# The last inverse stage on tiles of 64 rows and 32 columns, in half units

## The chip, the cores and the metric

The kernel runs on one core of a Trainium2 chip. The metric is the device time of one execution in microseconds (us). A core has a TensorE (PE, matrix products, with its weight loads shown apart as PEld), a VectorE (DVE), a ScalarE (ACT), a GpSimd (POOL) and a SyncE (SP), which here does nothing but issue DMAs. All run their own instructions in order and wait for each other by semaphores.

## The reference

One layer on 2048 tokens (L) of 640 channels (D). First a long convolution whose kernel comes from a diagonal state-space model (N = 128 states for each channel), then a gated feed-forward network (F = 1728), each behind a layer norm with a scale and a shift from a condition vector and each added through a gate:

```python
def A(u):                                   # [1, L, D]
    dt = exp(log_dt); A = -exp(log_A_real) + 1j * A_imag; C = (C_real + 1j * C_imag) * dt[:, None]
    K = 2 * einsum("dn,dnl->dl", C, exp((A * dt[:, None])[:, :, None] * pos)).real
    y = irfft(rfft(u.T, 2L) * rfft(K, 2L), 2L)[:, :, :L].T
    return y + u * D_skip
def B(x):
    return (silu(x @ w1) * (x @ w3)) @ w2
sa, ca, ga, sb, cb, gb = split(silu(c) @ w_mod)
x = x + ga * A(layernorm(x) * (1 + ca) + sa)
x = x + gb * B(layernorm(x) * (1 + cb) + sb)
```

Everything is in fp32.

## The kernel before, in words

**First phase (0 to about 395 us).** The convolution is a transform of 4096 points in stages, forward for the tokens and for the generated kernel K, a product, and an inverse transform. Each stage is a set of matmuls with a constant table (`wk`, `wb`, `wz`, `wd`). The channels run in five pieces of 128. The work is cut in tasks, and a list of task numbers, `ORDER`, written out in the file, says in which order they are issued; the costs and due times that stand at the tasks are not read by `run`. The last product of the inverse's first stage, `fz`, is copied by ACT to `zt` and stored by SP to a buffer `zd` in HBM; the last stage reads it back with the other axes in front.

**The last inverse stage.** A token's place is 32 values long in one axis; the 64 positions of the other axis are grouped as `j`, 0 to 15, in four quarters `q`. `inverse_load` fetches `z` for `nj` values of `j` (I call each a token row below): for each of two pairs `pr` a tile whose upper 64 rows are quarter 2·pr and whose lower 64 rows are quarter 2·pr + 1, four DMAs in all. `inverse` then makes, for each token row and each cut of up to 512 columns, one PSUM tile `iy` of 128 rows with two matmuls, one for each pair, on tiles of 128 rows and 64 columns of the array. The table `wd` holds a block diagonal for them: a quarter's 64 rows have values in its own 32 columns and zeros in the 32 of the other quarter. DVE then adds `iy` into `x2`, which holds the layer's input x and, after this, the input of the second half.

All this stands in one SBUF tile `low`: the table, `x2[0]`, and two buffers of `z`, taken in turn by units of two token rows. Units 0 and 1 (token rows 0 to 3) are done in the plan for the first 512 channels, as tasks `iz0`, `iz1` (the loads) and `ir0`, `ir1` (the matmuls, additions and layer norm statistics). Their last 128 channels, four token rows in one load on SP and ACT, follow behind the plan, with `awake` matmuls as a filler for PE around them.

**The feed-forward network.** Blocks 0 and 1 of 512 tokens run in `ffn`, blocks 2 and 3 together in `pair_up` and `pair_down`. A block goes through 14 slices m of F in the order 0, 13, 1, 2, ... 12. For each slice `up` makes two PSUM tiles `gu` (15 matmuls each; the half slice 13 has one tile); `gate` evaluates them on ACT and DVE into `ah`, `al`; `down` adds 15 matmuls into five accumulators `acc`. Each fp32 operand is split in a high and a low part (`wh`, `wl`, `xh`, `xl`, `w2h`, `w2l`), so there are three products where one stood. The weights come by SP as `wr` and `w2r` and are split by ACT and DVE. The tag `gu` has three PSUM banks, shared by `gu` and `iy`.

A function `between(b, m)` is called in each slice and puts other work in among these. For block 0 and m from 2 to 7 it calls `inverse_unit(m)`: the four loads of the unit (token rows 2m and 2m + 1, all 640 channels) and its four `iy` tiles, two cuts of 320 channels for each token row. The framework's scheduler makes PE's order from this program: it may put the accumulations of an earlier slice before, between or behind the `iy` matmuls.

SP issues DMAs in program order; a DMA that must wait for a buffer holds those behind it.

Of the kernel before, what the change touches and what calls it, by code (L numbers as in the profile page):

```python
# [10 lines left out]
F32 = mybir.dt.float32  # L11
# [7 lines left out]
P = 128  # L19
L = 2048  # L20
D = 640
# [76 lines left out]
def shape_tables():  # L98

    slot_t0 = np.array([32 + s if s < 32 else 63 - s for s in range(64)])  # L100
    t1, t0, f0, f1 = np.arange(32), np.arange(64), np.arange(32) + 0.5, np.arange(64)
    w = 2 * np.pi / 4096


    a = w * 64 * t1[:, None] * f0
    wk = np.zeros((4, 32, 2, 4, 32))
    for g in range(4):
        wk[g, :, :, g] = np.stack([np.cos(a), -np.sin(a)], 1)


    def second(a):
        c, s = np.cos(a), np.sin(a)
        return np.concatenate([np.concatenate([c, -s], -1), np.concatenate([s, c], -1)], 0)

    wb = np.stack([second(w * slot_t0[:, None] * (f + 64 * f1)) for f in f0], 1)

    a = w * 64 * f1[:, None] * t0
    c, s = np.cos(a), np.sin(a)
    wz = np.tile(np.stack([np.block([c, s]), np.block([-s, c])], 1), (2, 1, 1))

    wd = np.zeros((2, 32, 2, NJ, 2, 2, 32))
    a = w * (64 * t1[:, None] + t0) * f0[:, None, None]
    st = np.stack([np.cos(a), -np.sin(a)], 1) * 2 / 4096
    for q in range(4):
        wd[q % 2, :, :, :, q // 2, q % 2] = st[..., 16 * q:16 * q + 16].transpose(0, 1, 3, 2)
    return {k: np.ascontiguousarray(v.astype(np.float32)) for k, v in
            (("t_wk", wk.reshape(P, 2, P)), ("t_wb", wb), ("t_wz", wz), ("t_wd", wd.reshape(P, NJ, 2, 64)))}

# [32 lines left out]
class Plan:  # L161
# [4 lines left out]
    def add(self, name, eng, took, f, after=(), rank=0.0, port=False, take=(), give=(), table=None, dma=None):  # L166
        assert name not in self.tasks, name
        if not isinstance(eng, tuple):
            eng, f = (eng,), f and (lambda e, f=f: f())
        self.tasks[name] = (eng, f, tuple(after))  # L170
# [14 lines left out]
class K:  # L185
# [351 lines left out]
    def inverse_load(self, at, j0, nj, d0, d1, other=None):  # L537

        zv = self.zd.rearrange("f r t d -> (f r) t d")
        n = nj * (d1 - d0)  # L540
        z = [self.low[:, o:o + n].rearrange("p (j d) -> p j d", j=nj) for o in (at, at + (1280 if nj == 2 else 512))]
        for pr in range(2):
            for g in range(2):
                t0 = 16 * (2 * pr + g) + j0
                self.held_back((other if g and other else self.nc.sync).dma_start(z[pr][g * 64:(g + 1) * 64], zv[:, t0:t0 + nj, d0:d1]))
        return z

    def inverse(self, j0, nj, z, ps, tag, bufs, d0, d1):
        nc = self.nc
        w = d1 - d0  # L550
        for j in range(nj):
            for o, n in ((0, w),) if w <= 512 else ((0, 320), (320, 320)):
                py = ps.tile([P, 512], F32, name=f"iy{j0 + j}_{d0 + o}", tag=tag, bufs=bufs)
                for pr in range(2):
                    mm = nc.tensor.matmul(py[pr * 64:(pr + 1) * 64, :n], self.wd[:, j0 + j, pr, :], z[pr][:, j, o:o + n],  # L555
                                     start=True, stop=True, tile_position=(0, pr * 64))
                x2 = self.x2[(j0 + j) // 4][:, (j0 + j) % 4, d0 + o:d0 + o + n]
                nc.vector.tensor_add(x2, py[:, :n], x2)
        return mm

    hold = None

    def inverse_unit(self, u, ps, tag, bufs):
        z = self.inverse_load(4608 + u % 2 * 2560, 2 * u, 2, 0, D)
        self.inverse(2 * u, 2, z, ps, tag, bufs, 0, D)


    def split(self, H, Lo, v, eng):
# [483 lines left out]
    def run(self):  # L1052
        real = self.nc
        self.setup()
        c = self.const
# [4 lines left out]
        def open_(name, side=None, bufs=1, space=None):  # L1060
            scopes[name] = ExitStack()
            return self.pool(name, bufs=bufs, space=space, ctx=scopes[name], side=side)

        def close(*names):
            for n in names:
                scopes.pop(n).close()
# [15 lines left out]
        nc = self.nc = Engines(self, real)  # L1082
# [16 lines left out]
        b = NB - 1  # L1099
# [13 lines left out]
        add = plan.add  # L1113
# [5 lines left out]
        z = {}  # L1119
        W = self.W["tail"]  # L1120
# [11 lines left out]
        def load_z(u):  # L1132
            z[u] = self.inverse_load(4608 + u % 2 * 2560, 2 * u, 2, 0, cut)

        def first_rows(u):
            self.inverse(2 * u, 2, z[u], psg, "f", 3, 0, cut)
            for j in (2 * u, 2 * u + 1):
                self.ln_part(self.stats[0], self.x2[0], j, 0, KT - 1)
        for u in range(2):
            add(f"iz{u}", "SP", 0, lambda u=u: load_z(u), ["change", "fx"] + [f"z{b - 1}.{j}.o{f}" for j in range(4) for f in range(2)], W, dma=[262144] * 4)  # L1140
            add(f"ir{u}", "PE", 2.4, lambda u=u: first_rows(u), [f"iz{u}"] + [f"{x}{b}.{i}.e" for x in ("hh", "k") for i in range(8)], W + 25)
        plan.run()
        self.nc = real
# [8 lines left out]
        ps = open_("ps", space=PSUM)  # L1152
        x2 = [keep.tile([P, 4, D], F32, name=f"x2{b}") for b in (2, 3)]
# [3 lines left out]
        z = self.inverse_load(9728, 0, 4, cut, D, real.scalar)  # L1157
# [7 lines left out]
        def between(b, m):  # L1165
            if b == 0 and m in (2, 4):
                self.load_x2(m // 2 + 1)
            if b == 0 and 2 <= m < 8:
                self.inverse_unit(m, ps, "gu", 3)
            if b == 0 and m == 9:  # L1170
                self.gb_row(ps)
            if (b, m) == (1, 0):
                close("lp")
                xc = open_("xc")
                self.px = [xc.tile([P, 2, 2 if i < 5 else 1, 512], F32R, name=f"x3_{i}") for i in range(6)]
            if (b, m) in ((0, 8), (1, 4)):
                nxt[b + 1] = self.ln2(b + 1, pool, ps)
            if (b, m) == (1, 6):
                nxt[3] = self.ln_pair(*nxt[2], pool, ps)
            if b == 1 and 6 <= m < 12:  # L1180
                next(nxt[3])

        pend = self.ffn(nxt, wp, pool, ps, po, between)
        close("conv")
        pool = open_("pair", "right")
# [228 lines left out]
    def spectra_tasks(self, b):  # L1414
# [59 lines left out]
        for i in range(8):  # L1474
            t = W["w"](b, i)
            n = f"w{b}.{i}."
            j = 4 * b + i // 2 - FP
            first = [f"hh{b}.{x}.e" for x in range(8)] + ([f"w{b - 1}.{i}.x1"] if b else ["wb", "cols", "inv"])
            firstk = [f"k{b}.{x}.e" for x in range(8)]
            room = [f"z{j // 4}.{j % 4}.z"] if j >= 0 else []  # L1480
            add(n + "f", "PE", 1.0, lambda i=i: of(0, i), first, t, take=[("bank", 1)])
            add(n + "h", "ACT", .48, lambda i=i: hold(i), [n + "f"], t - q, give=[("bank", n + "f")])
            add(n + "k", "PE", 1.0, lambda i=i: of(1, i), firstk + room, t + .1, take=[("bank", 1)])
            add(n + "x0", "DVE", .61, lambda i=i: product(i, 0), [n + "k", n + "h"] + ([f"w{b}.{i - 1}.x0"] if i % 2 else []), t - q, take=[] if i % 2 else [("fp", 1)])
            add(n + "x1", "DVE", .61, lambda i=i: product(i, 1), [n + "x0"], t - q)
            add(n + "c", "DVE", .67, lambda i=i: both(i), [n + "x1"], t - q, give=[("bank", n + "k")])
            if i % 2 == 0:
                continue
            j = i // 2
            n = f"z{b}.{j}."  # L1490
            add(n + "z", "PE", 1.95, lambda j=j: inverse(j), [f"w{b}.{i - 1}.c", f"w{b}.{i}.c"], t + W["late"], take=[("bank", 1), ("bank", 1, "'")],
                give=[("fp", f"w{b}.{i - 1}.x0")])
            for f in range(2):
                kept = "hz" if (b, j, f) == (NB - 1, 3, 1) else "zt"
                add(n + f"v{f}", ("ACT", "DVE"), (.48, .61), lambda e, j=j, f=f: out(j, f, e), [n + "z"], t - q,
                    take=[(kept, 1)], give=[("bank", n + "z" + "'" * f)])
                add(n + f"o{f}", "SP", 0, lambda j=j, f=f: store(j, f), [n + f"v{f}"], t, dma=[262144], give=[(kept, n + f"v{f}")])
# [272 lines left out]
```

## Time and profile before

| | |
|---|---|
| median of 3 runs | 971.52 us (971.05 to 973.86) |
| the profiled execution, its own time | 970.77 us |
| its span, first to last instruction | 968.8 us |
| its mean granted TensorE clock | 0.966 |
| instructions | 20106 |
| iy matmuls of line 555 (units 2 to 7 and the last 128 columns) on the chain that ended last | 2% of the span |
| DMA, mean over the span | 117 GB/s |

Line 146 is a helper that records every operation of the plan, so groups of the first phase are told apart by their tiles. In timelines and chains each row has its start and its length in us; behind an instruction stand its output and inputs by the program's names, the tile of the array, and the shape; in brackets the idle time of the engine ahead of it and what ended that. An fp32 matmul is two instructions in the profile.

### The profile page before, as it was taken

What the parts mean: (1) busy time and instruction counts of PE and PEld (TensorE: products, weight loads), DVE (VectorE), ACT (ScalarE), POOL (GpSimd) and SP (SyncE); (2) the same over time, 40 slices, a digit from 0 to 9 for tenths busy, and PEclk for the clock granted to TensorE, in tenths of its full rate; (3) what the DMA queues carried; (4) which work ended last, traced back from release to release, by engine and by line L of the source; (5) the groups of instructions that cost most, each with busy time, mean ns of one, the idle gap of its engine ahead of it and who ended that gap; (6) DMA issues with size and microseconds to landing.
All of it is one profiled execution on the core that took longest, in us unless ns stands there. A gap on an engine that the chain in (4) does not pass through costs nothing.

```text
span 968.8 us, 20106 instructions
## 1 busy us (share of the span) xinstructions
PE 860.8 (89%) x8017; PEld 685.6 (71%) x8017; DVE 712.9 (74%) x1292; ACT 517.0 (53%) x874; POOL 336.1 (35%) x345
## 2 busy tenths in 40 slices
PE   2165767899999997899999999999999999999997
PEld 1033655787878773667778888888888888888875
DVE  7888999999999973657684365566467777765763
ACT  5878879979888830523143243345234444445331
POOL 2789998599999530100000000000213223300000
PEclk9585989999999998999999999999999999999999
DMA  9956526624140296987523353223131122122242
GB/s 241 236 175 213 119 59 169 161 68 111 37 99 25 72 276 184 233 203 189 136 82 91 100 148 111 82 82 109 28 82 55 55 54 55 42 82 90 85 152 82
DMA packets 122821, 113.18 MB, mean 117 GB/s; under 512 B 11752, under 2 KB 106472, under 8 KB 121320
## 3 DMA queue, kind: packets, MB, share of 16 engines
q1 hardware_dynamic: 121992, 110.99, 42.6%
q8 instruction: 63, 1.03, 0.5%
q10 hardware_dynamic: 736, 0.92, 0.3%
q14 instruction: 30, 0.25, 0.1%
HBM read 90.91 MB, written 20.97 MB: 115 GB/s over the span
## 4 chain that ended last, share of the span: by engine, by line
PE 66%; DVE 13%; DMA 7%; ACT 6%; issue 3%; POOL 3%; SPq 1%; DVEq 0%; ACTq 0%; POOLq 0%
PE acc L1024 17%; PE p L777 16%; PE gu L987 6%; PE gu L989 6%; PE gu L988 6%; DVE yy L146 3%; DMA xs<-in_x 3%; PE ps L146 2%; PE kps L146 2%; DVE fp L146 2%; ACT tr L146 2%; PE fz L146 2%; DVE xx L146 2%; PE iy L555 2%; DMA sp<-in_w_mod 1%
## 5 line engine op out<-in xcount | busy, mean ns | idle before, releaser
L987 PE MATMUL gu<-xh,wh 128*128 128x512 f32 x270 | 105.0, 394 | 0.9 <-ACT xh L569 0.7
L989 PE MATMUL gu<-xh,wl 128*128 128x512 f32 x270 | 105.4, 390 | 0.0
L988 PE MATMUL gu<-xl,wh 128*128 128x512 f32 x270 | 105.3, 390 | 0.0
L777 PE MATMUL p<-x,wch 128*128 128x512 f32 x312 | 92.7, 390 | 0.0
L796 POOL TENSOR_TENSOR ws<-wp 128x256 f32<-128x256 f32 x13 | 9.6, 739 | 229.8 <-DVE wcl L570 114.9
L146 POOL TENSOR_TENSOR yy<-e,e 128x512 f32<-128x512 f32 x80 | 87.1, 1103 | 3.0 <-PE kps L146 2.3
L146 POOL TENSOR_TENSOR ph<-p,p 128x1024 int32<-128x1024 int32 x40 | 78.5, 1964 | 16.1 <-ACT tr L146 15.7
L146 DVE TENSOR_TENSOR yy<-yy,tr 128x512 f32<-128x512 f32 (+1 forms) x80 | 75.1, 944 | 5.0 <-POOL yy L146 4.6
L681 ACT ACTIVATE wh<-wr 128x640 fp32r<-128x640 f32 x51 | 34.9, 731 | 63.3 <-PE gu L988 54.1
L146 PE MATMUL kps<-yy,xx 128*32 128x64 f32 x2560 | 49.7, 231 | 20.9 <-DVE xx L146 11.5
L777 PEld LDWEIGHTS p<-x,wch 128*128 128x128 f32 x312 | 58.3, 188 | 12.6 <-ACT s L812 0.4
L146 PEld LDWEIGHTS kps<-yy,xx 128*32 128x32 f32 x2560 | 43.4, 115 | 32.8 <-issue 17.0
L987 PEld LDWEIGHTS gu<-xh,wh 128*128 128x128 f32 x270 | 50.6, 188 | 11.7 <-ACT xh L569 1.0
L989 PEld LDWEIGHTS gu<-xh,wl 128*128 128x128 f32 x270 | 50.7, 188 | 11.1 <-DVE wl L690 0.4
L988 PEld LDWEIGHTS gu<-xl,wh 128*128 128x128 f32 x270 | 50.8, 188 | 10.4 <-DVE xl L570 0.2
L693 POOL MEMSET w2l<- 64x640 f32 x1 | 0.6, 633 | 163.7 <-PE acc L1024 163.7
L777 PE MATMUL p<-x,wcl 128*128 128x512 f32 x156 | 57.0, 390 | 0.0
L146 ACT ACTIVATE tr<-ph,hpi 128x512 f32<-128x512 f32 x80 | 54.6, 689 | 3.2 <-DVE yy L146 2.3
L146 DVE TENSOR_TENSOR xx<-tr,xx 128x512 f32<-128x512 f32 x80 | 54.3, 680 | 2.1 <-ACT tr L146 1.9
L814 DVE TENSOR_TENSOR s<-p,s 128x512 f32<-128x512 f32 x52 | 34.7, 682 | 26.9 <-ACT s L812 22.9
L146 PE MATMUL ps<-wk,ks 128*64 128x128 f32 x640 | 42.0, 285 | 13.7 <-DVE ks L146 9.6
L1000 ACT ACTIVATE th<-gu 128x512 f32<-128x512 f32 x26 | 15.5, 598 | 69.9 <-PE gu L989 69.8
(368 smaller groups left out, 2315.9 us busy)
## 6 DMA issues: line engine op xcount, KB each, us to landing
wr<-in_w SPq DMA_DIRECT2D x52, 320.0 KB, 3.8
zd<-zt SPq DMA_DIRECT2D x39, 256.0 KB, 2.7
w2r<-in_w SPq DMA_DIRECT2D x26, 320.0 KB, 3.2
wp<-in_w SPq DMA_DIRECT2D x26, 320.0 KB, 3.5
wq<-in_w SPq DMA_DIRECT2D x26, 320.0 KB, 3.2
low<-zd SPq DMA_DIRECT2D x24, 320.0 KB, 5.9
xs<-in_x SPq DMA_DIRECT2D x16, 320.0 KB, 10.0
hs<-hb SPq DMA_DIRECT2D x20, 256.0 KB, 2.9
```

What stands on the lines that cost most here:

```text
L146: self.prev = self.k.order(f(*a, **kw), self.prev)
L555: mm = nc.tensor.matmul(py[pr * 64:(pr + 1) * 64, :n], self.wd[:, j0 + j, pr, :], z[pr][:, j, o:o + n], start=True, stop=True, tile_positi ...
L681: self.nc.scalar.activation(wh[:, i], raw[:, i], AF.Copy)
L693: self.nc.gpsimd.memset(w2l[64:].bitcast(F32), 0.0)
L777: nc.tensor.matmul(to, t[:, o], y[:, k], start=start and k == i == 0, stop=stop and (k, i) == (n - 1, 2), skip_group_check=True)
L796: G.tensor_tensor(s[0], a21, a22, op=ALU.add)
L814: add = lambda o, bk, s: V.tensor_tensor(o, bk, s, op=ALU.add)
L987: nc.tensor.matmul(pg, wh[:, k, :], xh[:, k, :], start=(k == 0), stop=False)
L988: nc.tensor.matmul(pg, wh[:, k, :], xl[:, k, :], start=False, stop=False)
L989: nc.tensor.matmul(pg, wl[:, k, :], xh[:, k, :], start=False, stop=(k == KT - 1))
L1000: nc.scalar.activation(th, gu[0], AF.Tanh, scale=0.5)
L1024: nc.tensor.matmul(acc[k], *two(a, w), start=(m == 0 and i == 0), stop=(m == 12 and i == 2))
```

## The change

The table `wd` has the same shape, but for odd token rows p its two row halves are exchanged. `inverse_load` fetches even and odd token rows of a quarter apart: the even ones into the row half of before, the odd ones into the other, so eight DMAs of half the size where four stood. `inverse` takes two token rows at a time with a PSUM tile for each, and four matmuls for each tile, one for each quarter, on tiles of 64 rows and 32 columns; the zeros of the table are no longer read. Between them the two token rows use all eight such tiles of the array. The number of additions on DVE is the same.

In `ffn` a unit is done in two halves, one for each cut of 320 channels: half i = m − 2 for m from 2 to 7, i = m − 3 for m from 9 to 13, and the last, i = 11, at m = 0 of block 1. Unit 2 + i // 2 is loaded with its first half. The costs noted at the task of the loads (not read, as said) now name eight DMAs. The lines of the kernel move by 12 or so.

```diff
@@ -122,7 +122,8 @@
     a = w * (64 * t1[:, None] + t0) * f0[:, None, None]
     st = np.stack([np.cos(a), -np.sin(a)], 1) * 2 / 4096
     for q in range(4):
-        wd[q % 2, :, :, :, q // 2, q % 2] = st[..., 16 * q:16 * q + 16].transpose(0, 1, 3, 2)
+        for p in range(2):
+            wd[(q + p) % 2, :, :, p::2, q // 2, q % 2] = st[..., 16 * q + p:16 * q + 16:2].transpose(0, 1, 3, 2)
     return {k: np.ascontiguousarray(v.astype(np.float32)) for k, v in
             (("t_wk", wk.reshape(P, 2, P)), ("t_wb", wb), ("t_wz", wz), ("t_wd", wd.reshape(P, NJ, 2, 64)))}
 
@@ -541,28 +542,39 @@
         z = [self.low[:, o:o + n].rearrange("p (j d) -> p j d", j=nj) for o in (at, at + (1280 if nj == 2 else 512))]
         for pr in range(2):
             for g in range(2):
-                t0 = 16 * (2 * pr + g) + j0
-                self.held_back((other if g and other else self.nc.sync).dma_start(z[pr][g * 64:(g + 1) * 64], zv[:, t0:t0 + nj, d0:d1]))
+                for p in range(2):
+                    t0 = 16 * (2 * pr + g) + j0
+                    to = z[pr][(g ^ p) * 64:(g ^ p) * 64 + 64, p::2]
+                    self.held_back((other if g and other else self.nc.sync).dma_start(to, zv[:, t0 + p:t0 + nj:2, d0:d1]))
         return z
 
-    def inverse(self, j0, nj, z, ps, tag, bufs, d0, d1):
+    def inverse(self, j0, nj, z, ps, tag, bufs, d0, d1, part=None):
+
         nc = self.nc
         w = d1 - d0
-        for j in range(nj):
-            for o, n in ((0, w),) if w <= 512 else ((0, 320), (320, 320)):
-                py = ps.tile([P, 512], F32, name=f"iy{j0 + j}_{d0 + o}", tag=tag, bufs=bufs)
-                for pr in range(2):
-                    mm = nc.tensor.matmul(py[pr * 64:(pr + 1) * 64, :n], self.wd[:, j0 + j, pr, :], z[pr][:, j, o:o + n],
-                                     start=True, stop=True, tile_position=(0, pr * 64))
-                x2 = self.x2[(j0 + j) // 4][:, (j0 + j) % 4, d0 + o:d0 + o + n]
-                nc.vector.tensor_add(x2, py[:, :n], x2)
+        cuts = ((0, w),) if w <= 512 else ((0, 320), (320, 320))
+        for o, n in cuts if part is None else cuts[part:part + 1]:
+            for j in range(0, nj, 2):
+                py = [ps.tile([P, 512], F32, name=f"iy{j0 + j + p}_{d0 + o}", tag=tag, bufs=bufs) for p in range(2)]
+                for p in range(2):
+                    for q in range(4):
+                        r, c = 64 * ((q + p) % 2), 32 * q
+                        mm = nc.tensor.matmul(py[p][c:c + 32, :n], self.wd[r:r + 64, j0 + j + p, q // 2, c % 64:c % 64 + 32],
+                                              z[q // 2][r:r + 64, j + p, o:o + n], start=True, stop=True, tile_position=(r, c))
+                for p in range(2):
+                    i = j0 + j + p
+                    x2 = self.x2[i // 4][:, i % 4, d0 + o:d0 + o + n]
+                    nc.vector.tensor_add(x2, py[p][:, :n], x2)
         return mm
 
     hold = None
 
-    def inverse_unit(self, u, ps, tag, bufs):
-        z = self.inverse_load(4608 + u % 2 * 2560, 2 * u, 2, 0, D)
-        self.inverse(2 * u, 2, z, ps, tag, bufs, 0, D)
+    def inverse_half(self, i, ps, tag, bufs):
+
+        u, h = 2 + i // 2, i % 2
+        if h == 0:
+            self.zu = self.inverse_load(4608 + u % 2 * 2560, 2 * u, 2, 0, D)
+        self.inverse(2 * u, 2, self.zu, ps, tag, bufs, 0, D, h)
 
 
     def split(self, H, Lo, v, eng):
@@ -1137,7 +1149,7 @@
             for j in (2 * u, 2 * u + 1):
                 self.ln_part(self.stats[0], self.x2[0], j, 0, KT - 1)
         for u in range(2):
-            add(f"iz{u}", "SP", 0, lambda u=u: load_z(u), ["change", "fx"] + [f"z{b - 1}.{j}.o{f}" for j in range(4) for f in range(2)], W, dma=[262144] * 4)
+            add(f"iz{u}", "SP", 0, lambda u=u: load_z(u), ["change", "fx"] + [f"z{b - 1}.{j}.o{f}" for j in range(4) for f in range(2)], W, dma=[131072] * 8)
             add(f"ir{u}", "PE", 2.4, lambda u=u: first_rows(u), [f"iz{u}"] + [f"{x}{b}.{i}.e" for x in ("hh", "k") for i in range(8)], W + 25)
         plan.run()
         self.nc = real
@@ -1165,8 +1177,9 @@
         def between(b, m):
             if b == 0 and m in (2, 4):
                 self.load_x2(m // 2 + 1)
-            if b == 0 and 2 <= m < 8:
-                self.inverse_unit(m, ps, "gu", 3)
+            i = m - 2 if m < 8 else m - 3
+            if b == 0 and m >= 2 and m != 8 or (b, m) == (1, 0):
+                self.inverse_half(i if b == 0 else 11, ps, "gu", 3)
             if b == 0 and m == 9:
                 self.gb_row(ps)
             if (b, m) == (1, 0):
```

What the order makes of it is shown at three places. The first is on PE, around 420 us, where the accumulations of slice 13 (`acc` from `ah_13`) end. Before:

```order
L1024 MATMUL acc_5352<-w2h_13_5059,ah_13_5380 128x512
L1024 MATMUL acc_5352<-w2l_13_5077,ah_13_5380 128x512
L555 MATMUL iy_0_5471<-low 64x320 x2
L1024 MATMUL acc_5353<-ah_1_5448,w2h_1_5395 128x512
L1024 MATMUL acc_5349<-w2h_1_5395,ah_1_5448 128x512
L1024 MATMUL acc_5350<-w2h_1_5395,ah_1_5448 128x512
L1024 MATMUL acc_5351<-w2h_1_5395,ah_1_5448 128x512
L1024 MATMUL acc_5352<-w2h_1_5395,ah_1_5448 128x512
L555 MATMUL iy_320_5475<-low 64x320 x2
```

The same place after:

```order
L1036 MATMUL acc_5380<-w2h_13_5067,ah_13_5408 128x512
L1036 MATMUL acc_5380<-w2l_13_5085,ah_13_5408 128x512
L562 MATMUL iy_0_5496<-low 32x320 x3
L999 MATMUL gu_20_5522<-xh_5278,wh_2_5512 128x512
L1000 MATMUL gu_20_5522<-xl_5279,wh_2_5512 128x512
L1001 MATMUL gu_20_5522<-xh_5278,wl_2_5517 128x512
```

Behind the iy matmuls there stood the accumulations of slice 1; now the 30 gu matmuls of slice 2 stand there, and the accumulations of slice 1 come behind them. Of the half unit's eight matmuls the other five stand among those of slice 13.

The second place is on PE too, further on in block 0: where the gu matmuls of slice 3 end, before, and where the accumulations of slice 2 end, after. Before:

```order
L988 MATMUL gu_31_5586<-xl_5251,wh_3_5575 128x512
L989 MATMUL gu_31_5586<-xh_5250,wl_3_5580 128x512
L555 MATMUL iy_0_5649<-low 64x320 x2
L555 MATMUL iy_320_5653<-low 64x320 x2
L555 MATMUL iy_0_5657<-low 64x320 x2
L555 MATMUL iy_320_5661<-low 64x320 x2
L1024 MATMUL acc_5353<-ah_3_5634,w2h_3_5576 128x512
L1024 MATMUL acc_5353<-ah_3_5634,w2l_3_5581 128x512
```

After:

```order
L1036 MATMUL acc_5380<-w2l_2_5518,ah_2_5571 128x512
L1036 MATMUL acc_5380<-w2h_2_5513,al_2_5572 128x512
L562 MATMUL iy_0_5673<-low 32x320 x4
L562 MATMUL iy_0_5674<-low 32x320 x4
L999 MATMUL gu_40_5700<-xh_5278,wh_4_5690 128x512
L1000 MATMUL gu_40_5700<-xl_5279,wh_4_5690 128x512
```

A whole unit of four PSUM tiles stood there in one piece; now a half stands there, with two tiles of four matmuls each, between acc of slice 2 and gu of slice 4.

The third place is SP's queue in the last part of the first phase. `zd<-zt` are the stores, `low<-zd` the loads of units 0 and 1, `wr` and `w2r` the weights of slices 13, 1 and 2. Before:

```order
L146 DMA w2r_13_4930<-in_w 64x640 x2
L146 DMA low<-zd 64x2x512 x4
L665 DMA wr_1_5389<-in_w 128x5x128 x2
L146 DMA zd<-zt_5016 128x4x128
L670 DMA w2r_1_5392<-in_w 128x640
L146 DMA zd<-zt_5027 128x4x128
L146 DMA low<-zd 64x2x512 x4
L665 DMA wr_2_5479<-in_w 128x5x128 x2
L670 DMA w2r_2_5482<-in_w 128x640
L146 DMA zd<-zt_5074 128x4x128
L146 DMA zd<-zt_5114 128x4x128
```

After:

```order
L147 DMA w2r_13_4930<-in_w 64x640 x2
L147 DMA low<-zd 64x512 x8
L677 DMA wr_1_5417<-in_w 128x5x128 x2
L147 DMA zd<-zt_5016 128x4x128
L682 DMA w2r_1_5420<-in_w 128x640
L147 DMA zd<-zt_5031 128x4x128
L147 DMA low<-zd 64x512 x8
L147 DMA zd<-zt_5082 128x4x128
L147 DMA zd<-zt_5126 128x4x128
L677 DMA wr_2_5507<-in_w 128x5x128 x2
L682 DMA w2r_2_5510<-in_w 128x640
```

Each unit's four loads have become eight in the same place, and the weights of slice 2 have moved behind two stores.

## The prediction

> **What bounds the kernel now.** I read the page's first part, then the windows from 416 us on, then the chain of waits there, then single rows of the timeline.
>
> ```profile
> PE 860.8 (89%) x8017; PEld 685.6 (71%) x8017; DVE 712.9 (74%) x1292; ACT 517.0 (53%) x874; POOL 336.1 (35%) x345
> ...
> 416.00:424.00 8.00, 7.04 (x35) 3.66 (x33) 4.09 (x8) 3.25 (x5) 0.00 (x0) 1.00 0.78 199
> 424.00:440.00 16.00, 16.00 (x76) 11.58 (x75) 12.03 (x36) 3.33 (x6) 0.00 (x0) 1.00 0.80 214
> ...
> 460.00:480.00 20.00, 20.00 (x97) 14.28 (x94) 15.90 (x54) 3.70 (x6) 0.00 (x0) 1.00 0.63 165
> ```
>
> The columns of a window are its us, the busy time of PE, PEld, DVE, ACT and POOL with instructions, the granted clock, the DMA share and GB/s. In block 0 (from 424 us) PE is busy for every microsecond, at the full clock; DVE has 4.1 of 20 us to spare where it is fullest. So there a microsecond of PE work taken out moves the end by a microsecond. Just before, from 416 to 424, PE lacks 0.96 us: that is one wait, treated below. The inverse stage stands in this stretch as ten groups of iy matmuls: nine are on the chain of waits, the tenth (four instructions at 420.18) is just ahead of the wait.
>
> ```profile
> 416.49 1.23 PE iy L555 x8
> ...
> 423.33 0.69 PE iy L555 x4
> ...
> 433.35 1.77 PE iy L555 x12
> ...
> 437.63 0.69 PE iy L555 x4
> ...
> 446.52 2.30 PE iy L555 x16
> ...
> 459.24 1.76 PE iy L555 x12
> ...
> 463.52 0.69 PE iy L555 x4
> ...
> 472.41 2.30 PE iy L555 x16
> ...
> 485.14 2.45 PE iy L555 x16
> ```
>
> With those four they are 96 instructions: six units of 16, two instructions for each fp32 matmul.
>
> **Block 0, the PE work.** What a group costs is read from the start of the instruction before it to the start of one behind it, less what those instructions take alone (0.23 us each in the chain, 0.227 from 444.77 to 446.13 over six).
>
> ```profile
> 444.77 0.39 PE L989 MATMUL gu<-xh,wl 128*128 128x512 f32 x1
> ...
> 446.13 0.39 PE L989 MATMUL gu<-xh,wl 128*128 128x512 f32 x1
> 446.45 2.38 PE L555 MATMUL iy<-low 128*64 128x320 f32 x16
> 448.75 0.50 PE L1024 MATMUL acc<-ah,w2h 128*128 128x512 f32 x1
> 449.09 0.40 PE L1024 MATMUL acc<-ah,w2l 128*128 128x512 f32 x1
> ...
> 463.12 0.40 PE L1024 MATMUL acc<-w2l,ah 128*128 128x512 f32 x1
> 463.45 0.76 PE L555 MATMUL iy<-low 128*64 128x320 f32 x4
> 464.14 0.50 PE L1024 MATMUL acc<-al,w2h 128*128 128x512 f32 x1
> 464.48 1.11 PE L1024 MATMUL acc<-w2h,al 128*128 128x512 f32 x4
> ```
>
> A group of 16 costs 449.09 − 446.13 − 2 × 0.227 = 2.51 us, one of 4 costs 464.48 − 463.12 − 0.454 = 0.91. The 128x64 tiles run in pairs, so these are 8 rounds and 2 rounds: a round is (2.51 − 0.91)/6 = 0.267 us, and going into a group and out of it 0.91 − 0.534 = 0.38. Before: 48 rounds and 10 groups, 12.8 + 3.8 = **16.6 us**.
>
> After, a half unit has 8 matmuls on 8 different tiles, again 16 instructions of 320 columns. If all eight run together, that is 2 rounds. The order of after has 13 groups (12 halves, of which unit 2's first is cut in 5 and 3 matmuls), so 26 rounds. Whether eight run together no row shows; the nearest are these:
>
> ```profile
> 269.35 1.17 PE L146 MATMUL kps<-yy,xx 128*32 128x64 f32 x64
> ...
> 356.69 1.99 PE L146 MATMUL fz<-fp,wz 64*128 64x512 f32 x8
> ...
> 377.87 7.13 PE L146 MATMUL awake<-low,ident 128*128 128x512 f32 x16 [0.79 <-DVE low L146]
> ```
>
> An awake instruction uses the whole array: 7.13/16 = 0.446 us for 512 columns. Eight fz instructions on two tiles of 64 rows would take 3.57 one by one and take 1.99: 1.8 at a time. 64 kps instructions of 64 columns on four tiles of 32 columns would take 64 × 0.446/8 = 3.57 one by one and take 1.17: 3 at a time, held up by their issue, 1.17/64 = 0.018 us each. So row halves work side by side, and column quarters too; each kind of split alone. I take both together as working, with the issue of six further tiles at 0.018, 0.1 us per half. After: 26 × 0.267 + 13 × 0.38 + 12 × 0.1 = 6.9 + 4.9 + 1.2 = **13.1 us**; 3.5 us go. Bounds: 4.7 if the issue hides, and a loss in the rivals below, where the eight do not run together. DVE has as many additions of 128x320 as before, and each x2 block is whole before its layer norm.
>
> **The wait at 421 us.**
>
> ```profile
> 420.18 0.76 PE L555 MATMUL iy<-low 128*64 128x320 f32 x4
> 421.90 0.50 PE L1024 MATMUL acc<-ah,w2h 128*128 128x512 f32 x1 [0.96 <-ACT w2h L682]
> ...
> 419.10 1.60 ACT L681 ACTIVATE wh<-wr 128x640 fp32r<-128x640 f32 x2 [6.46 <-DMA wr<-in_w]
> ...
> 419.87 1.68 DVE L690 TENSOR_TENSOR wl<-wr,wh 128x640 fp32r<-128x640 f32 x2 [5.79 <-ACT wh L681]
> ```
>
> ACT has waited 6.46 us for the weights wr of step 2, and its w2h of step 1, which acc needs, is queued behind. In the changed order PE does not come to that acc after the iy group but to gu of step 2, 30 instructions, 6.8 us. Those need wh and wl, whose two parts run on ACT from 419.10 to 420.70 and on DVE from 419.87 to 421.55; the first parts are there when the iy group ends, near 420.9. The second gu tile takes its bank from iy, whose addition stands on DVE behind wl, so soon after 421.55, and the bank is due at 420.9 + 15 × 0.227 = 424.3. So the **0.96 us** go, and acc, due 6.8 us later, finds w2h ready. The bound on the other side: nothing is saved, if wr lands so much later that gu itself waits.
>
> **The first phase (352 to 396 us).**
>
> ```profile
> 353.80 2.59 SPq L146 DMA_DIRECT2D low<-zd  x4
> 356.49 2.08 SPq L665 DMA_DIRECT2D wr<-in_w  x2
> 358.67 1.05 SPq L146 DMA_DIRECT2D zd<-zt  x1
> ...
> 358.67 5.95 DMA zd<-zt
> ...
> 364.71 0.60 ACT L146 ACTIVATE zt<-fz 128x512 f32<-128x512 f32 x1 [5.38 <-DMA zd<-zt]
> 365.36 1.08 PE L146 MATMUL iy<-low 128*64 128x512 f32 x4 [2.85 <-ACT zt L146]
> ...
> zd<-zt SPq DMA_DIRECT2D x7, 256.0 KB, 3.5
> ...
> 426.49 2.37 SPq L545 DMA_DIRECT2D low<-zd  x4
> ```
>
> Unit 0's four loads stand on SP ahead of wr and of the store of zt, on which the chain goes on through ACT and PE. Eight loads of half the size cost, at the 2.37/4 = 0.59 us of a two-row load, 8 × 0.59 = 4.7 instead of 2.59 us: the store starts **2.1 us** later. Its cover is the queue in the DMA engines: it takes 5.95 us here, where the median store of this stretch takes 3.5, so 2.45 us are waiting behind earlier traffic, and a store that starts later waits less. I take 0; without the cover it is +2.1. PE's iy there saves nothing, since its second bank waits for the ACT zt. The last 128 columns:
>
> ```profile
> 380.20 1.52 ACTq L545 DMA_DIRECT2D low<-zd  x2
> ...
> 384.93 1.15 PE L555 MATMUL iy<-low 128*64 128x128 f32 x12
> 386.23 0.44 PE L555 MATMUL iy<-low 128*64 128x128 f32 x4 [0.15 <-DVE low L558]
> ```
>
> Four loads each on SP and ACT instead of two end 1.1 us later at 0.59 each; the filler awake, which ends at 384.93, covers some 0.5 of it. Against that the iy of four tokens, 1.74 us to the end of its second row, becomes some 0.9 with eight tiles. In unit 1 PE's part is shorter, but two DVE additions then stand in a row; I take nothing for it. I take **0** for the phase, with bounds from −1.0 (these small gains alone) to +3.2 (2.1 and 1.1, nothing covered). In block 0 the 24 additional loads, 24 × 0.59 = 14 us of SP time, are spread over 90 us; the load issued at 426.49, unit 4's, is used at 446.45, so 20 us of cover are there.
>
> **Sum.** 3.5 + 0.96 = 4.5 us of the profiled execution's 970.77 (span 968.8 and 2.0 around it): 966.3. That execution lies 0.75 under the median of the three runs, 971.52; from the median the sum is **967.0**.
>
> **Rivals.**
> 1. *Row halves of one bank take turns.* Each bank is written by two column quarters from the upper row half and two from the lower. If the halves of a bank alternate, a half unit has 4 rounds: 12 × (4 × 0.267 + 0.38) + 0.9 for the cut one = 18.3, 1.7 more than 16.6; less the 0.96 of the wait, +0.7: 972.2. For it: the fz tiles write different banks, so no row has a shared one. Against: within a bank the two halves write different partitions, and the kps quarters run 3 at a time into one tile.
> 2. *Slower: the turns are taken in queue order.* The matmuls of a token stand in the order upper, lower, upper, lower. If each waits for the one ahead in its bank, only the last of the first token and the first of the second overlap: 7 turns of two passes, 14 rounds, 12 × (14 × 0.267 + 0.38) + 0.4 = 49.8, 33.2 more than 16.6; less 0.96, about 1004. If merely two tiles run at a time, 8 rounds, it is 12 × 2.51 + 0.9 − 16.6 − 0.96 = +13.5, 985. The side changes near 4 rounds a half, and from five on it is slower by more than 0.3%.
> 3. *The first phase is not covered.* Store and last loads arrive late, +3.2: 970.2.
>
> The Trainium skill, "TensorEngine Tiling (Array Packing)", section "Restrictions and Gotchas", says that different row tiles cannot access the same PSUM bank at once and that software must see to it; that speaks for rivals 1 and 2, and by it the time would be 972 or 1004. The fz row agrees that two row tiles overlap with a bank each, and no run here shows a shared bank.
>
> **How the numbers follow.** The forecast, eight tiles together, has 0.64: both kinds of split are in the rows at near their full width, and the tiles share neither rows of a bank nor cells. Rivals 1, 2 and 3 have 0.12 each. About 0.3%, 2.9 us, is what a measurement here can tell from no change. The forecast's own range is 964.5 (issue hidden, small gains of the first phase) to 969.1 (2.1 us uncovered), a little of it within 0.3%: faster 0.62; same 0.25 (rivals 1 and 3 and that tail); slower 0.13 (rival 2 and mishaps). The range runs from 963.5 to 972.5: it leaves out rival 2 and some tails, under 0.2.
>
> **What would show it.** Right: iy groups of 16 instructions in about 0.6 to 0.8 us between gu and acc, thirteen in block 0 and the start of block 1; no idle PE from 416 to 500 us; gu at 421 with no wait; the ACT zt near 365 us no later than now. Wrong: iy groups of 1.2 us (rival 1), of 2.3 or 3.9 us (rival 2), or a start of block 0 that lies over 1 us later (rival 3). Not in the sum: a wait for a PSUM bank at a group, since a half takes two of the three banks at once and the gu behind it in PE's queue would stand, then acc.

## The result, and the profile after

The changed kernel takes 966.58 us (median of 5 runs, 964.0 to 968.26) beside 971.64 us for the one before: a ratio of 0.994, 95% interval 0.9916 to 0.9963, or 5.1 us less. 967.0 was forecast. Two more groups of runs gave 0.9942 (0.9920 to 0.9965) and 0.9961 (0.9946 to 0.9976). The profiled execution took 967.95 us, with a span of 966.0 at a mean clock of 0.964. In the last of these groups one run of the changed kernel (1733 us) and one of the kernel before (1036.5 us) were disturbed, and the ratios and means here leave them out.

The page's first line:

```profile
PE 856.0 (89%) x8145; PEld 681.2 (71%) x8145; DVE 713.6 (74%) x1292; ACT 518.4 (54%) x874; POOL 336.2 (35%) x345
```

The windows of the same stretch as before, with the same columns:

```profile
412.00:420.00 8.00, 8.00 (x43) 6.00 (x42) 4.31 (x7) 2.01 (x4) 0.00 (x0) 1.00 1.00 223
420.00:436.00 16.00, 16.00 (x89) 11.87 (x85) 10.15 (x20) 6.48 (x10) 0.00 (x0) 1.00 0.70 200
...
456.00:476.00 20.00, 20.00 (x114) 15.48 (x114) 13.33 (x41) 6.52 (x10) 0.00 (x0) 1.00 0.62 164
```

And the chain of waits at its beginning (start, us, engine, tile, line, instructions):

```profile
419.47 0.68 PE iy L562 x10
420.15 2.51 PE acc L1036 x10
422.66 0.67 PE iy L562 x6
...
433.74 0.70 PE iy L562 x16
```

PE has no gap from 412 us on, and the wait is gone. Sixteen inverse instructions take 0.70 us where sixteen took 2.30; since they are half a unit now and were a whole one before, a unit goes from 2.30 us to 1.40. All of block 0's and block 1's gain can be read from two places, the first gu matmul and the first matmul of `p`, with which blocks 2 and 3 begin. The timeline of PE before, then after:

```profile
395.04 0.96 PE L987 MATMUL gu<-xh,wh 128*128 128x512 f32 x3 [0.73 <-ACT xh L569]
...
695.60 0.39 PE L777 MATMUL p<-xh,wch 128*128 128x512 f32 x1
```

```profile
398.05 0.96 PE L999 MATMUL gu<-xh,wh 128*128 128x512 f32 x3 [0.73 <-ACT xh L581]
...
692.99 0.39 PE L789 MATMUL p<-xh,wch 128*128 128x512 f32 x1
```

That stretch goes from 300.56 to 294.94 us, 5.62 less. It is the same to 0.1 us in the two other profiles of the changed kernel (294.96 and 294.87). But it begins 3.0 us later in this execution: 1.85 of that are there ahead of any changed instruction (already the fz matmuls of 341.67 us start at 343.52, and those of 356.69 at 358.55; in the two other profiles the latter start at 357.92 and 355.11, so this part is scatter), and 1.15 come in the last part of the first phase. The tables below use two stretches: A, from that fz group to the first gu, and B, from the first gu to the first p.

### The profile page after: what moved, and what is told of

It is laid out like the page before. It is cut to its first block, busy times and chain, and to the rows that moved or that the text cites. A ratio compares the mean times of both kernels' runs of the same rounds, so it can differ in the third digit from the quotient of the medians.

```text
span 966.0 us, 20403 instructions
## 1 busy us (share of the span) xinstructions
PE 856.0 (89%) x8145; PEld 681.2 (71%) x8145; DVE 713.6 (74%) x1292; ACT 518.4 (54%) x874; POOL 336.2 (35%) x345
## 4 chain that ended last, share of the span: by engine, by line
PE 57%; DVE 2%; DMA 2%; ACT 1%; issue 0%; SPq 0%; DVEq 0%; ACTq 0%
PE p L789 17%; PE acc L1036 16%; PE gu L999 7%; PE gu L1001 6%; PE gu L1000 6%; DMA wq<-in_w 1%; PE iy L562 1%; PE awake L147 1%; PE q L789 1%; PE tp L613 1%; PE fz L147 1%; DMA zd<-zt 0%; PE acc L147 0%; DVE w2l L988 0%; PE iy L147 0%; DVE wq L983 0%
## 5 line engine op out<-in xcount | busy, mean ns | idle before, releaser
L147 PE MATMUL ps<-wk,xb 128*64 128x128 f32 x640 | 46.8, 297 | 5.3 <-DVE hb L147 2.5
L1014 DVE TENSOR_TENSOR a<-a,gu 128x512 f32<-128x512 f32 x26 | 17.9, 687 | 45.5 <-PE gu L1001 45.4
```

What stands on the lines that cost most here:

```text
L147: self.prev = self.k.order(f(*a, **kw), self.prev)
L1014: nc.vector.tensor_mul(a, a, gu[1])
```

## The experiments

Two groups of questions: what makes B shorter, and what A costs. The change in all of them is against the changed kernel, unless it says otherwise.

### The change with the tiles of before

```diff
-                    for q in range(4):
-                        r, c = 64 * ((q + p) % 2), 32 * q
-                        mm = nc.tensor.matmul(py[p][c:c + 32, :n], ..., tile_position=(r, c))
+                    for pr in range(2):
+                        mm = nc.tensor.matmul(py[p][pr * 64:(pr + 1) * 64, :n], self.wd[:, j0 + j + p, pr, :], z[pr][:, j + p, o:o + n], ..., tile_position=(0, pr * 64))
```

with the table and the four loads of before as well.

> The half units of the change, but with the tables, loads and 128x64 tiles of before. Theory (tiles save rounds, the order saves the wait): 12 groups of 4 rounds, 12 x (0.38 + 1.07) = 17.4 us instead of 16.8, the 0.96 us wait at 421 us gone, the first phase as before: 971.6 + 0.6 - 1.0 = 971.2. Rival (the spread itself brings the gain, the tiles little): 967 to 968.

Measured: 972.75 us, ratio 1.0011 (0.9997 to 1.0024). B is 300.27 us, 0.3 less than before where 0.4 was expected. The timeline of PE has a half in

```profile
444.15 1.30 PE L558 MATMUL iy<-low 128*64 128x320 f32 x8
```

that is, four rounds, 1.23 us to the next instruction, and PE waits for w2h nowhere in block 0. So the spread alone removes the wait and gives it back in more groups. The time is 1.5 us over the 971.2 of the theory; in the profile A is 39.5 us, 1.2 more than before's, although the loads are those of before.

### The change without the exchange of row halves

```diff
-                        r, c = 64 * ((q + p) % 2), 32 * q
+                        r, c = 64 * (q % 2), 32 * q
```

with the table and the loads of before.

> The change without the exchange of row halves (table and four loads as before), so that both token rows use the same four tiles of 64x32. Theory (as many matmuls at once as there are tiles, a bank shared by two row halves costs nothing): 4 rounds a half, about 1.45 us for a group of 16, 12 x 1.45 = 17.4 us in block 0, no wait at 421, first phase as before: about 971.3. Rival (row halves that share a bank take turns): 8 rounds a half, 2.5 us for a group, about 984.

Measured: 973.16 us, ratio 1.0017 (0.9999 to 1.0034), 1.9 us over the theory; B is 300.48 us and A, in the profile, 41.2. The timeline, for this kernel and then for the changed one:

```profile
447.40 1.28 PE L559 MATMUL iy<-low 64*32 64x320 f32 x16
```

```profile
444.81 0.77 PE L562 MATMUL iy<-low 64*32 64x320 f32 x16
445.50 0.50 PE L999 MATMUL gu<-xh,wh 128*128 128x512 f32 x1
445.84 0.39 PE L1000 MATMUL gu<-xl,wh 128*128 128x512 f32 x1
```

Sixteen instructions of one shape: 1.21 us to the next instruction when four tiles share them, 0.70 when eight do. Four rounds against two, with a round of (1.21 − 0.70)/2 = 0.26 us. The starts of the single instructions, which the timeline lumps together, show the rounds themselves: in the changed kernel eight start between 444.805 and 444.852 us and the other eight between 445.099 and 445.145; in this kernel four start at a time (from 447.402, 447.695, 447.964 and 448.234 us). In both kernels a bank is written by both row halves, each into partitions of its own, and they take no turns. Rival 1 (1.45 us a group with eight tiles) and rival 2 (over 2.3) have fallen. The Trainium skill, "TensorEngine Tiling (Array Packing)", section "Restrictions and Gotchas", has row tiles never in one bank at the same time; where they write different partitions of it the runs here show no cost in time, and the measurement decides.

### The change with every inverse matmul issued twice

```diff
-                    for q in range(4):
+                    for q in (0, 1, 2, 3, 0, 1, 2, 3):
```

It does the inverse stage's products twice, with the same results.

> The change with every inverse matmul issued twice into the same tile. Theory (eight tiles at once, a round of 320 columns 0.267 us, the rest of a group entry and exit): a group of 32 instructions takes 0.70 + 0.53 = 1.23 us from its first start to the next instruction, block 0 and 1 grow by 12 x 0.53 = 6.4 us. Rival (the group is held by its issue, 16 instructions in 0.70 us): 32 instructions in about 1.4 us, growth about 8.4 us.

One run, 980.24 us. Groups of 32 instructions take 1.26 to 1.34 us to the next instruction (the timeline of this kernel):

```profile
439.41 1.33 PE L562 MATMUL iy<-low 64*32 64x320 f32 x32
```

B grows by 7.1 us, between the two expectations (6.4 and 8.4) and nearer to the first: the two additional rounds take (1.26 − 0.70)/2 = 0.28 to (1.34 − 0.70)/2 = 0.32 us each. A group held by its issue would have taken 1.4 us. So the issue is almost hidden, not the limit.

### Whole units instead of halves

```diff
-            i = m - 2 if m < 8 else m - 3
-            if b == 0 and m >= 2 and m != 8 or (b, m) == (1, 0):
-                self.inverse_half(i if b == 0 else 11, ps, "gu", 3)
+            if b == 0 and 2 <= m < 8:
+                self.inverse_half(2 * m - 4, ps, "gu", 3)
+                self.inverse_half(2 * m - 3, ps, "gu", 3)
```

> The change, but whole units at m from 2 to 7, both halves one behind the other. Theory: fewer places but cut groups again (its order has 11 groups, some with a single token row of four tiles), about 13.3 us of iy work instead of the 12.2 measured with halves, and the wait of about 1 us at 421 comes back: 966.6 + 2.1 = 968.7. Rival (the spread brings nothing, the tiles all): 966.6.

Measured: 973.79 us, ratio 1.0020 (1.0004 to 1.0036), worse than both expectations. B is 299.93 us, 5.0 more than with halves. The waits of PE from 419 to 500 us (who waits, for whom, us in total, times, longest) show where:

```profile
PE acc L1036 <- ACT w2h L694: 1.0, 1, 1.0
PE gu L999 <- DVE x L567: 0.6, 1, 0.6
PE iy L562 <- DVE x L567: 0.5, 2, 0.4
```

```profile
435.94 1.37 PE L562 MATMUL iy<-low 64*32 64x320 f32 x24
437.70 0.74 PE L562 MATMUL iy<-low 64*32 64x320 f32 x8 [0.39 <-DVE x L567]
```

The wait for w2h is back, as the theory had it. What it left out: four iy tiles want four banks where `gu` has three, so with faster matmuls PE now waits for DVE's additions (1.1 us in the list), and a token row that is left over has only four tiles to itself, so that a unit is done in more rounds. This is the larger part: counted from their first start to the next instruction, without waits, the 13 groups cost 12.2 us here and 9.2 with halves. So the tiles without the spread make B 0.6 us shorter than before, the spread without the tiles 0.3, and both together 5.6: the halves, two banks each, are what lets the faster tiles be used. The rest of the time lies, in this profile, in the first phase (its A is 41.84 us, 2.3 more than the change's in the first profile) and is taken up at the end.

### Eight loads: the kernel before with them, the change with four, the change with sixteen

A unit's two token rows can be exchanged with four loads, if one DMA takes a row of each quarter (17 or 15 rows apart) and the lower half holds its two rows the other way round:

```diff
-                for p in range(2):
-                    t0 = 16 * (2 * pr + g) + j0
-                    to = z[pr][(g ^ p) * 64:(g ^ p) * 64 + 64, p::2]
-                    self.held_back((other if g and other else self.nc.sync).dma_start(to, zv[:, t0 + p:t0 + nj:2, d0:d1]))
+                for i in range(0, nj, 2):
+                    src = zv[:, 32 * pr + j0 + i + g:32 * pr + j0 + i + g + 1, d0:d1]
+                    ap = [list(x) for x in src.ap]
+                    src = bass.AP(tensor=src.tensor, offset=src.offset, ap=[ap[0], [(15 if g else 17) * zv.ap[1][0], 2], ap[-1]])
+                    to = z[pr][g * 64:g * 64 + 64, i:i + 2]
+                    self.held_back((other if g and other else self.nc.sync).dma_start(to, src))
...
-                                              z[q // 2][r:r + 64, j + p, o:o + n], start=True, stop=True, tile_position=(r, c))
+                                              z[q // 2][r:r + 64, j + (1 - p if r else p), o:o + n], start=True, stop=True, tile_position=(r, c))
```

> The change, but with two rows of z fetched by one DMA again (strides of 17 and 15 rows; the exchanged half holds its two rows the other way round): four loads for a unit, as before. Theory (the first phase lost 1.15 us to SP's additional loads): about 1.2 us less than the change, 965.4, and unit 0's store starts about 2 us earlier after the loads. Rival (that 1.15 us is the scatter of executions, like the 1.85 us that the changed kernel's profile lost ahead of 340 us, where nothing is changed): 966.6.

> The change with merged loads once more, beside the change itself. Theory (eight loads cost 1.6 us at unit 0, as the profiles of the change and of the whole units show it against three kernels with four): 1.2 to 1.6 us less than the change. Rival (something else on the way takes the place of the store): no difference.

> The changed kernel once more, beside the others of this group. Both theories: ratio to before about 0.9945, some 5.3 us less.

The other way, the kernel before with a DMA for each token row (its four loads in a loop over p, `zv[:, t0 + p:t0 + nj:2, d0:d1]` into `z[pr][g * 64:g * 64 + 64, p::2]`):

> The kernel before with nothing changed but its loads: one DMA for each token row of a quarter, eight a unit, no exchange. Theory (the additional loads cost time in the first phase alone): 1.2 to 1.6 us more than before, the stretch from the first gu matmul on as before. Rival (the DMA queue covers them): no difference from before.

And the change with the eight loads of units 0 and 1 cut once more, at 32 rows:

> The change with sixteen loads for each of units 0 and 1 (32 rows each), nothing else altered. Theory (SP's load issues hold the stores behind them, and that is on the way): eight loads took 5.9 us on SP where four took 2.6, so sixteen take 9 to 12, and the way from unit 0's last fz before it to the next fz, 14.7 us with eight, 13.3 with four, becomes 17 to 20; with unit 1 the time grows by 3 to 6 us over the change. Rival (what unit 0 loses is covered later, as the time of the kernel with merged loads, no less than that of the change, suggests): under 1 us more than the change.

| kernel | loads of a unit | time, ratio to before | unit 0: fz to next fz | A | B |
|---|---|---|---|---|---|
| before | 4 | | 13.23 | 38.35 | 300.56 |
| before with single rows | 8 | 973.16, 1.0009 (0.9993 to 1.0024) | 14.39 | 39.78 | 300.99 |
| change | 8 | 966.47, 0.9942 (0.9920 to 0.9965) | 14.84, 14.72, 15.08 | 39.50, 39.46, 41.74 | 294.94 |
| change, merged loads | 4 | 966.7, 0.9950 (0.9935 to 0.9965) | 13.20 | 37.96 | 294.92 |
| the same again | 4 | 966.86, 0.9943 (0.9924 to 0.9962) | 12.65 | 37.43 | 294.95 |
| change, 16 loads for units 0 and 1 | 16 | 969.64, 0.9969 (0.9953 to 0.9986) | 14.70 | 43.71 | 294.97 |

(The columns in us are differences of starts in the profiles. The change's three values are of its three profiles.) Five more profiles belong beside the table. With four loads, unit 0 takes 13.7 us in the change with the tiles of before, 13.5 without the exchange, and 13.2 and 13.6 in the two kernels of the next section; with eight it takes 14.8 in the kernel with whole units. To four and eight loads, then, unit 0 answers as the theory has it: 12.7 to 13.7 us and 14.4 to 15.1. A doesn't separate them as well: in the same five profiles it is 39.5, 41.2, 37.9, 38.7 and 41.8 us, so that a kernel with four loads can have as long an A as the change. SP's queue, ACT and PE in the changed kernel:

```profile
355.78 5.91 SPq L147 DMA_DIRECT2D low<-zd  x8
361.79 1.10 SPq L677 DMA_DIRECT2D wr<-in_w  x2
362.99 0.47 SPq L147 DMA_DIRECT2D zd<-zt  x1
...
367.22 0.60 ACT L147 ACTIVATE zt<-fz 128x512 f32<-128x512 f32 x1 [6.04 <-DMA zd<-zt]
367.87 1.93 PE L147 MATMUL iy<-low 64*32 64x512 f32 x8 [3.47 <-ACT zt L147]
```

the window around that iy:

```profile
366.00:370.00 4.00, 1.93 (x8) 0.20 (x8) 0.05 (x1) 0.60 (x1) 0.00 (x0) 0.60 1.06 335
```

and with merged loads:

```profile
354.34 2.60 SPq L147 DMA_DIRECT2D low<-zd  x4
357.04 1.66 SPq L679 DMA_DIRECT2D wr<-in_w  x2
358.80 0.80 SPq L147 DMA_DIRECT2D zd<-zt  x1
...
364.87 0.60 ACT L147 ACTIVATE zt<-fz 128x512 f32<-128x512 f32 x1 [5.35 <-DMA zd<-zt]
365.51 1.06 PE L147 MATMUL iy<-low 64*32 64x512 f32 x8 [2.21 <-ACT zt L147]
```

Counted from the fz group (358.55 and 356.88), the store is issued at 4.44 with eight loads and at 1.92 with four, 2.5 us later. ACT, which waits for it, starts at 8.67 and at 7.99, 0.7 later: it goes on 4.2 us after the store's issue instead of 6.1, and 1.8 of the 2.5 us are covered. The other 0.9 us is PE's: the same eight instructions take 1.93 us instead of 1.06, in a window with a granted clock of 0.60. That this comes of the loads is not shown: in the kernel before with single rows PE idles 3.87 us ahead of the same iy, longer than the 3.47 here, and takes 1.15.

The time, however, doesn't show unit 0's 1.5 us. The runs of the change have a mean of 966.8 us (16 runs, standard error 0.4), those with merged loads 966.8 (20 runs, 0.4). The kernel before with eight loads is 0.9 us slower, with an interval that holds zero, and the 1.2 to 1.6 us of the theory as well. With sixteen loads the kernel is 2.6 us slower than the change (0.0027 of 972, from two groups of runs whose intervals overlap; the means of the runs, 969.4 and 966.8, say the same), which is neither the theory's 3 to 6 us nor the rival's under 1. And it is not in unit 0, which takes 14.70 us where 17 to 20 were expected: the store is issued later still, 5.85 us after fz, but ACT starts at 8.34, no later than with eight loads. A is 4.2 us longer than in the change's first profile at another place, where the last 128 columns' loads come too late for PE (timeline):

```profile
385.44 2.60 SPq L551 DMA_DIRECT2D low<-zd  x4
...
387.96 0.58 PE L565 MATMUL iy<-low 64*32 64x128 f32 x4 [1.66 <-DMA low<-zd]
388.72 0.47 PE L565 MATMUL iy<-low 64*32 64x128 f32 x2 [0.17 <-DMA low<-zd]
389.35 2.06 PE L565 MATMUL iy<-low 64*32 64x128 f32 x26 [0.16 <-DMA low<-zd]
```

and the window of their end, with a granted clock of 0.50:

```profile
390.00:394.00 4.00, 4.00 (x27) 1.87 (x24) 3.09 (x17) 0.00 (x0) 0.00 (x0) 0.50 0.44 113
```

That these loads are late because of SP's load issues, as the theory would have it, is not shown. Counted from fz they are issued at 29.3 us instead of 25.2, and the chain has them wait there for the last store of zt to land, for 5.22 us. In this kernel the scheduler also put the weights of slices 1 and 2 behind unit 1's loads, nearer to these stores, and part of the 4.2 us is the low clock; the runs don't separate the three. At eight loads, the profiles show 1.5 us in unit 0 and the times show none of it to within about 1 us. What takes its place in executions without a profile stays open.

### No cut group: the halves one step later

With merged loads, the halves start at step 3 (i = m − 3 up to m = 13, then i = 11 in block 1). The steps m of `between` count from 0 in the order of the slices, so that step 2 is slice 1.

> The kernel with merged loads, its twelve halves at steps 3 to 13 of block 0 and step 0 of block 1, so that none is cut in two and none stands ahead of gu of slice 2. Theory (the weights wr of slice 2, whose ACT part starts 24.5 to 25 us after the first gu matmul, are what PE would wait for there; the cut group is hidden under that): PE waits 3 to 4 us at gu of slice 2, with acc of slice 13 now behind that wait, and the time is 2 to 3.5 us more than with the halves from step 2. Rival (the cut group costs its 0.9 us of PE time and nothing waits): 0.9 us less.

Measured: 967.78 us, ratio 0.9947 (0.9926 to 0.9969). B is 295.34 us, 0.4 more than with merged loads alone, so that neither expectation holds. The expected wait isn't there. The gu of slice 2 runs at once, while ACT's `wh` behind the long wait for `wr` comes 3 us after (timelines of PE and ACT of this kernel):

```profile
414.45 0.39 PE L1001 MATMUL gu<-xh,wh 128*128 128x512 f32 x1
...
417.46 1.55 ACT L695 ACTIVATE wh<-wr 128x640 fp32r<-128x640 f32 x2 [6.69 <-DMA wr<-in_w]
```

So that `wr` is slice 3's; slice 2's weights had been split before. The theory has fallen, and so has a detail of the prediction, below. In place of the cut group a new wait has come, behind the half at step 8, whose additions and statistics stand on DVE ahead of the layer norm of block 1:

```profile
490.32 0.50 PE L1001 MATMUL gu<-xh,wh 128*128 128x512 f32 x1 [0.80 <-DVE v L620]
```

The last version leaves step 8 out, as the change does, and does the last two halves at steps 0 and 1 of block 1 (what `between` does behind the last half moves to step 1 with it):

> Merged loads, the halves at steps 3 to 7 and 9 to 13 of block 0 and steps 0 and 1 of block 1: none cut in two, and none at step 8, where the kernel with halves from step 3 to 13 got a new wait of 0.80 us on DVE at the next gu. Theory (without that wait the saved group shows): the stretch from the first gu to the first p 294.2 to 294.4 us (294.94 in the change), the first phase as in the other kernels with merged loads, so 0.6 to 2 us less than the change beside it. Rival (another wait takes its place): 294.9 or more, and no less than the change.

> The changed kernel once more, to be compared with the kernel beside it. Both theories: ratio to before 0.994 to 0.995.

Measured: 965.67 us, ratio 0.994 (0.992 to 0.996), beside 967.56 us and 0.9961 (0.9946 to 0.9976) for the change in the same group; the intervals overlap. B is 294.98 us, no less than with the change: the order has cut the last half instead, so that there are 13 groups again. The rival had B right, but not for its reason: no wait took the place of the one at step 8, a cut did. Neither of the two versions can be told from the change by its time.

## Why the prediction was right

**The bound.** From 424 us on before, and from the first gu on after, PE waits for nothing in block 0 beyond the 0.7 us at that gu, and what was taken out of its work came off B: 4.7 us of groups (below) and the 0.96 of the wait, where B is 5.62 shorter.

**The PE work of the inverse.** 3.5 us were forecast, with a bound of 4.7 if the issue of eight tiles is hidden. It is hidden: 0.70 us for 16 instructions on eight tiles, 0.69 for four instructions on two (463.45 to 464.14 before). The term of 12 × 0.1 us for the issue was too much; without it the sum is 4.7, and with the 0.96 of the wait 5.66, where 5.62 was measured. The group's price from the rows of after, 445.84 − 444.49 − 2 × 0.227 = 0.90 us (the accumulation ahead of it starts at 444.49), is that of two rounds, 0.91.

**The wait at 421 us.** It went, in every kernel with the spread, and stayed with whole units. The cover was named rightly (30 gu matmuls ahead of the accumulation of slice 1), and so was ACT's queue. The weights were named wrongly: the text took the `wr` that ACT waited for as the one which the next gu needs, and so had a near race between PE and `wh`. It belongs to slice 3, and the gu that covers the wait had its weights long before. The 0.96 us do not depend on that.

**The first phase.** Nothing net was taken, with bounds from −1.0 to +3.2; 1.15 us came in this execution. The terms: SP's store 2.5 us later (2.1 forecast), 1.8 of it covered, since the store lands sooner after its issue (all was taken as covered, up to 2.45); 0.9 us for PE at a lower clock, which the sum had not; a gain of 0.4 to 0.5 at the last 128 columns behind the filler (from the first filler matmul to the first of the second filler 8.73 before and 8.37 after, and 0.1 more up to the layer norm's transposes; about 0.8 was forecast for PE's part there). The kernels with four and eight loads say that unit 0's 1.5 us come with the loads, but not that the time has them. Two of the prediction's own signs failed here: the ACT zt near 365 us comes 0.65 us later, counted from fz (8.67 us instead of 8.02), and block 0 starts 1.15 us later even when the scatter ahead of fz is left out.

**The rivals.** 1 and 2 fell with the 0.70 us. 3, the uncovered first phase, was right in part in the profile, too little to turn the forecast.

**The sum.** −4.5 us from 971.52 gave 967.0; 966.58 was measured. The mechanism, eight tiles together and no wait, is shown; that the number is so close is luck in part, since two errors of 1.2 us (issue) and some 1 us (first phase, in the profile) stand against each other. The lower end of the forecast's own range, 964.5, should by its terms have been 967.0 − 1.2 − 1.0 = 964.8.

## What to carry to other kernels

Before a matmul with structural zeros is kept for its simplicity, count how many tiles of the array its non-zero blocks would fill at the same time; here exchanging the row halves of every other row made a set of eight out of two sets of four that collide, and halved the rounds at once. Faster work in short groups brings up what was hidden behind it: the banks and the left-over rows (whole units waited for DVE and took more rounds, halves did not), the price of going into and out of a group (0.38 of its 0.91 us here), and the transfers that got more numerous. What an edit does in a stretch far from it, here in unit 0 of the first phase, is seen only if the profile is cut at fixed instructions and compared stretch by stretch over several profiles; whether the time has it, only the times say, and here they don't show it.

## What was not expected of the hardware

The clock that the throttle grants falls in the first phase around times in which PE idles, and with the same idle time ahead it is granted in one execution and not in the next. The 20 transposes ahead of the first gu, in two executions of the changed kernel (two further profiles). The timeline of the one and of the other:

```profile
394.25 2.41 PE L613 MATMUL tp<-ident,xn 128*128 128x128 f32 x20 [2.34 <-ACT xn L597]
```

```profile
392.22 3.90 PE L613 MATMUL tp<-ident,xn 128*128 128x128 f32 x20 [2.33 <-ACT xn L597]
```

and the windows of both, the granted clock third from the end:

```profile
394.20:397.40 3.20, 2.42 (x21) 2.19 (x21) 1.77 (x4) 2.17 (x4) 0.00 (x0) 1.00 0.99 211
```

```profile
392.20:396.80 4.60, 3.90 (x20) 3.67 (x20) 1.72 (x3) 2.07 (x4) 0.00 (x0) 0.66 1.03 218
```

1.5 us between two executions of one program, as much as the effect that the loads were tested for; the same happened in the profiles of the kernel without the exchange and of the whole units (4.07 us), which is 1.7 us of what their A has more. PE was idle 2.33 or 2.34 us ahead in all of them, so that this idle time alone does not decide it; what does, the traces don't show. It may be part of why runs of one kernel differ by 4 us.
